# A Fourier transform along the tokens, followed by an expert layer: rows split by parity in place of halves

## The chip, the cores and the metric

The kernel runs on one core of one Trainium2 chip. The metric is the device time of one execution in microseconds, the median of several runs. Engines are named as in the profile: PE is TensorE (PEld its weight loads), DVE is VectorE, ACT is ScalarE, POOL is GpSimd, SP is SyncE, whose queue issues most DMA transfers.

## What is computed

The input x has 8 batches of 3072 tokens and 256 features, all in fp32; the weights come as float64.

```python
X = np.fft.fft(x, axis=1); X = np.fft.fft(X, axis=2)
x = X.real.astype(np.float32).reshape(8 * 3072, 256)
h = x @ w_in                                  # 256 x 2048
sp = np.where(h > 20.0, h, np.log1p(np.exp(np.minimum(h, 20.0))))
out = (h * np.tanh(sp)) @ w_out               # 2048 x 256
```

## The kernel before

**Tiling.** The 3072 tokens are taken as 3 x 1024. The transform of length 3 is made with additions, the one of length 1024 with matmuls against a table of cosines and sines (dft). The 1024 rows are folded to 256 with sums and differences (pair L332, sums L348 to L353, last_fold L362): tiles F0e, F1e, F0o, F1o, where "e" holds sums over features and "o" differences, and the digit c names one of two **halves** of the rows (0 to 127, and 256 down to 129). Row 128 has no partner. It is handled apart: make_mids (L627) computes its folds from a small tile ymid; put_mids (L374) places them by DMA in row 0 of fold tiles, nine transfers a batch; add_mid (L459) adds the rest.

**Even and odd frequencies.** For even frequencies the two halves are added before the matmul, for odd ones subtracted (over_c, L364, adds and subtracts the halves of the folds for one of the parities of each kind). A call of transform (L421) makes the cosine or sine sum of one parity into one PSUM tile: for even frequencies two matmuls of 128 and 130 columns (L429, L431), for odd ones two of 256 columns (L426), accumulated. The profile shows each of these fp32 matmuls as two passes.

**Chunks and steps.** The results of a batch are made as three chunks, each of 1024 tokens and 256 features, in the order first_chunk (L467), other_chunks (L491) and last_chunk (L521); each chunk is split into a high and a low part (split_to, L453: ScalarE copies the high part h, VectorE or GpSimd subtracts to get the low part l) for matmuls in reduced precision. The chunk is then multiplied with 16 blocks of the hidden layer, one block a step. A step (tau, L938 on) issues: six matmuls into pa and pb (mm1, L828 to L830); twelve matmuls of the output layer for the step six before (mm2, L869); make_h on VectorE (L837 to L839), which reads pa and pb; ScalarE's copy gh and GpSimd's difference gl of the step four before (L847, L848); ScalarE's Mish (L959). The first 12 steps use a plain fp32 path for mm2 (L860).

**What sets the order.** Every engine works its queue in the order in which the program issues. A batch has 48 steps. Steps 1, 2, 5 and 7 call other_chunks (steps 12 to 15 in batch 0), steps 17 and 18 last_chunk, steps 10 to 44 spread the folds of the next batch (fold_ops, L385, with a cost written by hand for each part), and steps 44 and 45 call first_chunk for the next batch, even and odd frequencies. pa and pb have two PSUM buffers each, and mm1 and the transforms take them in turn. So a transform's VectorE work has to be through before mm1 comes round to the same buffer.

**The start.** Batch 0's work before and among the first steps, and the conversion of the float64 weights (conv), stand in a list written by hand (EARLY, L153): entries with -1 come before step 0. chunk0 (L806) makes batch 0's first chunk, fold_z (L772) its folds, col_z (L672) and col_cs (L687) the same transforms for feature 0 of all batches, first_p0 (L705) that of batch 0 broadcast to all rows, and warm runs matmuls on zeros. The small arrays (ymid, ysel, eye, xcol in one tile, loaded) come on ACT's DMA queue (L724), the rest on SP's (L726 to L732).

Of the kernel before, what the change touches and what calls it, by code (L numbers as in the profile page):

```python
# [27 lines left out]
EVEN = list(range(2, 511, 4)) + list(range(0, 513, 4))  # L28
ODD = list(range(1, 512, 2))
NE = 258  # L30

DT = 2 * NE + 4 * 256
COLS0 = EVEN[:256] + ODD
COLS2 = EVEN[:128] + EVEN[129:] + ODD

# [30 lines left out]
def _layout(x, w_in, w_out):  # L66
# [6 lines left out]
    rows = np.array([[[_rows(n1, w, sg, 256 - m if c else m) for sg in range(2)] for n1 in range(3)]  # L73
# [3 lines left out]
    mids = np.array([_rows(n1, w, sg, 128) for w in range(2) for n1 in range(3) for sg in range(2)])  # L77
# [6 lines left out]
        "mid": np.ascontiguousarray(ym).reshape(12 * NB, D + 1),  # L84
# [5 lines left out]
def _tables():  # L90
# [10 lines left out]
    ev, od = np.array(EVEN), np.array(ODD)  # L101
    ae = 2 * np.pi * ((p[:, None] * ev[None, :]) % N2) / N2
    dft = np.zeros((128, DT))
    dft[:, :257] = np.cos(ae)
    dft[:, NE:NE + 257] = np.sin(ae)

    dft[0, :NE] *= 0.5
    dft[0, NE:2 * NE] = 0.0
    dft[0, NE:NE + 128] = np.sin(2 * np.pi * ((128 * ev[:128]) % N2) / N2)
    for c, m in enumerate((p, 256 - p)):  # L110
        ao = 2 * np.pi * ((m[:, None] * od[None, :]) % N2) / N2
        a8 = 2 * np.pi * ((128 * od) % N2) / N2
        o = 2 * NE + 512 * c
        dft[:, o:o + 256] = np.cos(ao)
        dft[:, o + 256:o + 512] = np.sin(ao)
        dft[0, o:o + 256] = np.cos(a8) if c else 0.5
        dft[0, o + 256:o + 512] = 0.5 * np.sin(ao[0]) if c else np.sin(a8)
# [6 lines left out]
    ysel = np.concatenate([np.kron(np.concatenate([f1, k * f1]), eye) for f1 in (fe, fo) for k in (1, -1)], 1)  # L124
# [9 lines left out]
SMALL = (D + 1, 12 * NB, 128, 24 * NB)  # L134
# [18 lines left out]
EARLY = [  # L153
    (-1, 'warm', (2,)),
# [24 lines left out]
    (-1, 'col_z', (0,)),  # L179
# [5 lines left out]
    (-1, 'chunk0', (1, 2)),  # L185
    (-1, 'pairs0', (0, 0, 'o')),
# [60 lines left out]
def fft_moe(ctx, tc, x, w_in, w_out, small_d, cs_d, dft_d, out, single_d):  # L247
# [28 lines left out]
    alt = cp.tile([128, NE], F32, name="alt")  # L276
# [19 lines left out]
    mid0 = small(1, 3 * 128, 2)  # L296
    loaded = small(128, sum(SMALL))
    ymid, ysel, eye, xcol = (loaded[:n, sum(SMALL[:i]):sum(SMALL[:i + 1])] for i, n in enumerate((12 * NB, 12 * NB, 128, 128)))
    xcol = xcol.rearrange("p (c w i b) -> p c w i b", c=2, w=2, i=6)
    xt = small(128, 12 * NB).rearrange("p (k c q b) -> p k c q b", k=2, c=2, q=3)  # L300
    xm = small(1, 6 * NB).rearrange("p (k q b) -> p k q b", k=2, q=3)
# [5 lines left out]
    mid_d = dp.tile([6 * NB, 2, 128], F32, name="mid_d")  # L307
# [13 lines left out]
    def fold_part(b, c, y, i, par):  # L321
        if par == 0 and c == 1:
            return folds[b][y, "-"] if (b, i) == (0, 0) else folds[b][1, y, 0][:, 0, 3 + i]
        return folds[b][c, y][:, par if COSINE[y][i] else 1 - par, i]
# [39 lines left out]
    def over_c(b, y, eng, lo=0):  # L364

        st, ops = folds[b], []
        ka = 0 if y == "e" else 1
        for k, i, j in ((ka, lo, 2), (1 - ka, 2, 3)):
            f0, f1, d = st[0, y][:, k, i:j], st[1, y][:, k, i:j], st[1, y, 0][:, 0, 3 + i:3 + j]
            ops.append(lambda f0=f0, f1=f1, d=d: eng.tensor_tensor(d, f0, f1, op=ALU.subtract))  # L370
            ops.append(lambda f0=f0, f1=f1: eng.tensor_tensor(f0, f0, f1, op=ALU.add))
        return ops

    def put_mids(b):  # L374


        for c, par, k, parts in ((0, 1, 0, (("o", 0), ("e", 2), ("o", 1))), (0, 0, 1, (("o", 0), ("e", 2), ("o", 1))),
                                 (1, 1, 1, (("e", 0), ("e", 1), ("o", 2)))):
            for y, i in parts:
                if b or i:  # L380
                    q, h = (i, 0) if y == "e" else ((i + 1) % 3, 1)
                    r = (3 * k + q) * NB + b
                    SP.dma_start(out=fold_part(b, c, y, i, par)[0:1], in_=mid_d[r:r + 1, h, :])

    def fold_ops(b):  # L385
# [20 lines left out]
        cross = []  # L406
        for i in range(4):
            def two(i=i):
                if i == 0:
                    cross.extend(zip(over_c(b, "e", V), over_c(b, "o", G)))  # L410
                for f in cross[i]:
                    f()
            steps.append((1.0, two))
# [3 lines left out]
    def const(c, par, sine):  # L417
        o = NE * sine if par == 0 else 2 * NE + 512 * c + 256 * sine
        return dft[:, o:o + (NE if par == 0 else 256)]

    def transform(dst, lhs, par, sine, mid_lhs=None, halves=(0, 1)):  # L421


        if par:
            for c in halves:
                T.matmul(dst, lhs(c), const(c, par, sine), start=c == 0, stop=c == 1)  # L426
        elif 1 in halves:
            t = const(0, 0, sine)
            T.matmul(dst[:, :128], lhs(1 - sine), t[:, :128], start=True, stop=True)  # L429
            d = dst[:, 128:NE]  # L430
            T.matmul(d, lhs(sine), t[:, 128:], start=True, stop=mid_lhs is None)  # L431
            if mid_lhs is not None:
                T.matmul(d, mid_lhs, alt[0:1, 128:], start=False, stop=True)
# [33 lines left out]
    def first_chunk(b, par, part=(0, 1, 2)):  # L467
# [10 lines left out]
        if 2 in part:  # L478
            if par == 0:
                new_chunk(ch)  # L480
# [542 lines left out]
```

## Time and profile before

| | |
|---|---|
| median of 3 runs | 1643.74 us (1643.66 to 1644.84) |
| profiled execution | 1645.03 us, span 1643.2 us |
| mean granted clock of TensorE | 0.995 of full |
| busy share PE, DVE, ACT, POOL | 99%, 66%, 52%, 70% |
| first step's first matmul | 35.02 us |

The span runs from the first to the last instruction. The timeline views give the start and the duration of instructions in us, and in brackets the idle time of the engine before one, with what ended it. Matmuls are pipelined: each shows some 0.17 us more than the time until the next may start, so the time a matmul costs is read from start to start.

### The profile page before, as it was taken

How to read it: one execution, taken by the hardware profiler on the slowest of the kernel's cores; microseconds unless marked ns; L12 is line 12 of the kernel's file. 1: busy time of each engine (PE TensorE's matmuls, PEld its weight loads, DVE VectorE, ACT ScalarE, POOL GpSimd, SP SyncE). 2: the span in 40 equal slices, each digit the busy share in tenths (PEclk: the TensorE clock that was granted, in tenths of full speed). 3: DMA queues.
4: the chain of work that ended last, by engine and by line, in shares of the span. 5: the costliest groups of instructions: out<-in, count | busy, mean ns of one | idle time of the engine just before them, and what ended most of it. 6: DMA issues, size and time to landing. Idle time of an engine off the chain costs nothing.

```text
span 1643.2 us, 20689 instructions
## 1 busy us (share of the span) xinstructions
PE 1629.2 (99%) x7484; PEld 1389.9 (85%) x7484; DVE 1085.3 (66%) x1612; ACT 849.9 (52%) x936; POOL 1148.4 (70%) x660
## 2 busy tenths in 40 slices
PE   8999999999999999999999999999999999999999
PEld 4557888888888888888888888888888888888887
DVE  6887776667666676676766767667766667664453
ACT  3445555555555555555554555555555555454454
POOL 2629876787658785687856886578865888565566
PEclk9999999999999999999999999999999999998999
DMA  5522002000030000300102000300002000000000
GB/s 240 206 77 90 1 33 93 17 32 27 7 110 0 33 26 7 109 33 1 33 24 86 33 3 31 109 1 33 26 7 109 23 11 27 7 33 26 7 27 26
DMA packets 24863, 74.96 MB, mean 46 GB/s; under 512 B 2981, under 2 KB 3106, under 8 KB 23738
## 3 DMA queue, kind: packets, MB, share of 16 engines
q1 hardware_dynamic: 24474, 73.03, 12.2%
q8 instruction: 60, 0.98, 0.3%
q10 hardware_dynamic: 288, 0.61, 0.1%
q14 instruction: 41, 0.34, 0.1%
HBM read 48.35 MB, written 25.27 MB: 45 GB/s over the span
## 4 chain that ended last, share of the span: by engine, by line
PE 94%; DVE 4%; DMA 1%; issue 0%; POOL 0%; ACT 0%; SPq 0%; DVEq 0%; POOLq 0%; ACTq 0%
PE acc L869 59%; PE pb L829 5%; PE pb L828 5%; PE pb L830 5%; PE pa L828 5%; PE pa L830 5%; PE pa L829 5%; PE pb L426 1%; PE pa L426 1%; PE acc L860 1%; DMA wring<-w_in_dram 0%; DMA swol<-w_in_dram 0%; DVE hring L838 0%; DMA hring<-small_dram 0%; DVE hring L837 0%
## 5 line engine op out<-in xcount | busy, mean ns | idle before, releaser
L848 POOL TENSOR_TENSOR gl<-hring,gh 128x1024 fp32r<-128x1024 f32 x372 | 887.2, 2385 | 409.1 <-ACT gh L847 404.1
L847 ACT CAST gh<-hring 128x1024 fp32r<-128x1024 f32 x372 | 389.7, 1048 | 659.1 <-PE acc L869 645.3
L869 PE MATMUL acc<-gh,woh 128*128 128x512 f32 x1488 | 564.9, 380 | 0.0
L869 PE MATMUL acc<-gh,wol 128*128 128x512 f32 x1488 | 564.8, 380 | 0.0
L837 DVE SCALAR_TENSOR_TENSOR hring<-p0b,wc,pa 128x512 f32<-128x512 f32 x384 | 286.4, 746 | 369.1 <-PE pa L830 359.6
L959 ACT ACTIVATE hring<-hring 128x1024 f32<-128x1024 f32 x384 | 404.2, 1053 | 41.6 <-DVE hring L839 41.6
L869 PE MATMUL acc<-gl,woh 128*128 128x512 f32 x1488 | 394.3, 379 | 0.0
L869 PEld LDWEIGHTS acc<-gl,woh 128*128 128x128 f32 x1488 | 281.6, 189 | 40.4 <-POOL gl L848 0.2
L869 PEld LDWEIGHTS acc<-gh,wol 128*128 128x128 f32 x1488 | 281.7, 189 | 40.4
L869 PEld LDWEIGHTS acc<-gh,woh 128*128 128x128 f32 x1488 | 281.7, 189 | 40.2
L838 DVE TENSOR_TENSOR hring<-hring,pb 128x512 f32<-128x512 f32 x384 | 264.0, 688 | 42.3 <-PE pb L830 1.4
L839 DVE TENSOR_TENSOR hring<-hring,pb 128x512 f32<-128x512 f32 x384 | 263.6, 686 | 13.3
L828 PE MATMUL pa<-h,wch 128*128 128x512 f32 x384 | 155.5, 405 | 0.0
L829 PE MATMUL pa<-l,wch 128*128 128x512 f32 x384 | 145.9, 380 | 1.2 <-DVE l L455 1.2
L828 PE MATMUL pb<-h,wsh 128*128 128x512 f32 x384 | 146.0, 380 | 0.8 <-ACT h L454 0.4
L829 PE MATMUL pb<-l,wsh 128*128 128x512 f32 x384 | 145.9, 380 | 0.3 <-POOL l L455 0.3
L830 PE MATMUL pa<-h,wcl 128*128 128x512 f32 x384 | 145.8, 380 | 0.0
L830 PE MATMUL pb<-h,wsl 128*128 128x512 f32 x384 | 145.8, 380 | 0.0
L829 PEld LDWEIGHTS pa<-l,wch 128*128 128x128 f32 x384 | 72.8, 190 | 12.5 <-issue 1.7
L828 PEld LDWEIGHTS pa<-h,wch 128*128 128x128 f32 x384 | 72.7, 189 | 12.2 <-issue 1.1
L828 PEld LDWEIGHTS pb<-h,wsh 128*128 128x128 f32 x384 | 72.7, 189 | 12.2 <-PE pa L830 1.2
L829 PEld LDWEIGHTS pb<-l,wsh 128*128 128x128 f32 x384 | 72.7, 189 | 10.9 <-POOL l L455 0.6
(275 smaller groups left out, 1163.5 us busy)
## 6 DMA issues: line engine op xcount, KB each, us to landing
xring<-x_dram SPq DMA_DIRECT2D x32, 768.0 KB
out_dram<-ot SPq DMA_DIRECT2D x96, 256.0 KB
p0b<-p_d SPq DMA_DIRECT2D x23, 256.0 KB
swoh<-w_in_dram SPq DMA_DIRECT2D x2, 1024.0 KB
swoh<-w_out_dram SPq DMA_DIRECT2D x2, 1024.0 KB
xring<-w_out_dram SPq DMA_DIRECT2D x2, 1024.0 KB
swol<-w_out_dram SPq DMA_DIRECT2D x2, 1023.5 KB
wring<-w_out_dram SPq DMA_DIRECT2D x2, 1023.5 KB
```

Of the source, the lines that this page charges most:

```text
L426: T.matmul(dst, lhs(c), const(c, par, sine), start=c == 0, stop=c == 1)
L828: T.matmul(dst, wh[:, fs], mixed(q[n + "h"]), start=True, stop=False)
L829: T.matmul(dst, wh[:, fs], mixed(q[n + "l"]), start=False, stop=False)
L830: T.matmul(dst, wl[:, fs], mixed(q[n + "h"]), start=False, stop=True)
L837: V.scalar_tensor_tensor(h[:, 0:512], p0b[ch], wc0[:, f:f + 1], pa, op0=ALU.mult, op1=ALU.add)
L838: V.tensor_tensor(h[:, 512:1024], h[:, 0:512], pb, op=ALU.add)
L839: V.tensor_tensor(h[:, 0:512], h[:, 0:512], pb, op=ALU.subtract)
L847: A.copy(gh, h)
L848: G.tensor_tensor(gl, h, gh, op=ALU.subtract)
L860: T.matmul(acc[i], w[:, o:o + 128], h[:, 512 * t:512 * t + 512], start=f == 0, stop=False)
L869: T.matmul(o, wout(w, f)[:, 128 * d:128 * d + 128], v, **kw)
L959: A.activation(hring[:, tau % RH], hring[:, tau % RH], AF.Mish)
```

## The change

Rows are split by **parity** (c = 0: rows 0, 2, 4, ...; c = 1: rows 1, 3, 5, ...) in place of halves. The transform of the even and of the odd rows is then made apart, each for half of the frequencies (130 columns for even frequencies, 128 for odd ones), side by side in one PSUM tile; the other half follows as sum and difference of the two (butterfly). over_c goes; put_mids has three transfers a batch. Batch 0's first chunk, col_z, col_cs and first_p0 use another routine (direct), which lets TensorE accumulate sums and differences, with negated folds (negs, xneg). In the start all loads become entries of EARLY, the small arrays first on SP's queue; col_z(0) moves behind chunk0. The diff, cut to its core:

```diff
+NQ = (130, 128)
+DT = 4 * sum(NQ)
...
-SMALL = (D + 1, 12 * NB, 128, 24 * NB)
+SMALL = (D + 1, 6 * NB, 128, 24 * NB)
...
 EARLY = [
+    (-1, 'load', ('small', 'S')),
+    (-1, 'load_w', ('in', 0)),
+    (-1, 'load', ('cs', 'A')),
+    (-1, 'load', (0, 'S')),
+    (-1, 'load', (1, 'S')),
+    (-1, 'load', ('dft', 'S')),
+    (-1, 'load', (2, 'S')),
+    (-1, 'load', (3, 'S')),
+    (-1, 'load_w', ('in', 1)),
     (-1, 'warm', (2,)),
...
-    (-1, 'col_z', (0,)),
     (-1, 'fold_z', (1,)),
     (-1, 'conv', ('out', 0, 0)),
     (-1, 'chunk0', (0, 1)),
     (-1, 'chunk0', (0, 2)),
     (-1, 'chunk0', (1, 1)),
     (-1, 'chunk0', (1, 2)),
+    (-1, 'col_z', (0,)),
...
     def put_mids(b):
-        for c, par, k, parts in ((0, 1, 0, (("o", 0), ("e", 2), ("o", 1))), (0, 0, 1, (("o", 0), ("e", 2), ("o", 1))),
-                                 (1, 1, 1, (("e", 0), ("e", 1), ("o", 2)))):
+        for y, i in (("o", 0), ("e", 2), ("o", 1)):
...
     def transform(dst, lhs, par, sine, mid_lhs=None, halves=(0, 1)):
+        n = NQ[par]
+        for c in halves:
+            mid = mid_lhs is not None and (par, sine, c) == (0, 0, 0)
+            T.matmul(dst[:, n * c:n * c + n], lhs(c), const(c, par, sine), start=True, stop=not mid)
...
+    def direct(dst, lhs, par, sine, mid_lhs=None, halves=(0, 1)):
+        n = NQ[par] - 1 + par
+        d = dst[:, :2 * n].rearrange("p (k s) -> p k s", k=2)
+        def twice(v):
+            return v[:, None, :].to_broadcast([v.shape[0], 2, n])
+        if 0 in halves:
+            T.matmul(d, lhs(0, False), twice(const(0, par, sine, 0, n)), start=True, stop=False)
+            if mid_lhs is not None and (par, sine) == (0, 0):
+                T.matmul(d, mid_lhs, twice(alt[0:1, :n]), start=False, stop=False)
+        if 1 in halves:
+            for k in (1, 0):
+                T.matmul(d[:, k], lhs(1, k == 0), const(1, par, sine, 0, n), start=False, stop=k == 0)
+
+    def butterfly(eng, dst, a, b, par, last=False):
+        lo, hi = (0, 128) if par else (0, 129) if last else (1, 129)
+        m = hi - lo
+        eng.tensor_tensor(dst[:, 0:m], a[:, lo:hi], b[:, lo:hi], op=ALU.subtract)
+        lo, hi = (1, 128) if last and not par else (0, 128)
+        eng.tensor_tensor(dst[:, m:256], a[:, lo:hi], b[:, lo:hi], op=ALU.add)
...
+    def first_chunk(b, par):
...
+        transform(pa, lambda c: fold_part(b, c, "e", 0, par), par, 0)
+        transform(pb, lambda c: fold_part(b, c, "o", 0, par), par, 1)
...
+        for k, p in enumerate((pa, pb)):
+            a = fp.tile([128, NQ[0]], F32, tag=f"base{k}", name="base")
+            both = fp.tile([128, 256], F32, tag=f"both{k}", name="both")
+            if k == par == 0:
+                add_mid(a[:, None, :n], p[:, None, :n], 0, b)
+                V.tensor_tensor(ends[:, b:b + 1], a[:, 0:1], p[:, n:n + 1], op=ALU.subtract)
+            else:
+                A.copy(a[:, :n], p[:, :n])
+            butterfly(V, both, a, p[:, n:2 * n], par)
+            split_to(q["pq"[k] + "h"][:, par], q["pq"[k] + "l"][:, par], both, V)
...
     def other_chunks(b, par, odd):
...
+        base = fp.tile([128, 2 * NQ[0]], F32, tag="base", name="base")
         if par == 0:
-            add_mid(base, pa, 1 + odd, b)
+            add_mid(base[:, None, :n], pa[:, None, :n], 1 + odd, b)
+            V.tensor_copy(base[:, n:2 * n], pa[:, n:2 * n])
         else:
-            V.tensor_copy(base[:, :n], pa[:, :n])
+            V.tensor_copy(base[:, :2 * n], pa[:, :2 * n])
         scaled, plain = (base, pb) if odd else (pb, base)
-        V.scalar_tensor_tensor(spare, scaled[:, :256], R3 if odd else -R3, plain[:, :256], op0=ALU.mult, op1=ALU.add)
...
-        split_to(q[h][:, par], q[l][:, par], spare, G)
-        V.scalar_tensor_tensor(full2[odd][:, sl].rearrange("p (a s) -> p a s", s=128), later(scaled, par),
-                               -R3 if odd else R3, later(plain, par), op0=ALU.mult, op1=ALU.add)
+        both = fp.tile([128, 256], F32, tag="both0", name="both")
+        for k, eng in ((0, V), (1, G)):
+            t = fp.tile([128, 2 * NQ[0]], F32, tag=f"turn{k}", name="turn")
+            V.scalar_tensor_tensor(t[:, :2 * n], scaled[:, :2 * n], R3 if odd != k else -R3, plain[:, :2 * n],
+                                   op0=ALU.mult, op1=ALU.add)
+            butterfly(eng, full2[odd][:, sl] if k else both, t, t[:, n:2 * n], par, k)
+        split_to(q[h][:, par], q[l][:, par], both, G)
...
     def make_mids():
...
-        for i, (o, v) in enumerate(((n + NB, od), (n + 4 * NB, od), (3 * NB, ev))):
-            T.matmul(pb[0:1, 128 * i + 128:128 * i + 256], ysel[:, o:o + 1], v, start=True, stop=True)
+        T.matmul(pb[0:1, 128:256], ysel[:, n + NB:n + NB + 1], od, start=True, stop=True)
...
-    G.memset(alt, 0.0)
...
-    A.dma_start(out=loaded, in_=small_d)
...
     def fold_z(c):
...
-            if c:
-                k = 0 if y == "e" else 1
-                f0, f1, d = folds[0][0, y][:, k, 0], folds[0][1, y][:, k, 0], eo[:, i, 0]
-                V.tensor_tensor(d, f0, f1, op=ALU.subtract)
-                V.tensor_tensor(f0, f0, f1, op=ALU.add)
...
+            for k, y in enumerate("eo"):
+                negs[y] = fp.tile([128, 2, 128], F32, tag=f"turn{k}", name="neg")
+                A.mul(negs[y], folds[0][1, y][:, :, 0], -1.0)
```

## Rows read from the trace of the kernel before

**Rows 1.** The page, part 1: engine, busy us (share), instructions.

```profile
PE 1629.2 (99%) x7484; PEld 1389.9 (85%) x7484; DVE 1085.3 (66%) x1612; ACT 849.9 (52%) x936; POOL 1148.4 (70%) x660
```

**Rows 2.** Chain in order of time, 400 to 425 us: start, us, what.

```profile
403.13 0.22 PE pa L828
...
407.01 0.22 PE pa L828
```

**Rows 3.** The same chain, 0 to 110 us.

```profile
0.73 6.17 DMA hring<-small_dram
```

**Rows 4.** Line L459: count, min/median/max ns, first and last start us, form.

```profile
L459 DVE SCALAR_TENSOR_TENSOR base<-alt,midc,pa x24: 472/483/486, 33.2 to 1442.9; 128x258 f32<-128x258 f32 x24
```

**Rows 5.** TensorE's timeline, even transform: start, us, line, op, out<-in, count.

```profile
1401.88 0.38 PE L429 MATMUL pa<-dft,e 128*128 128x128 f32 x2
...
1402.98 0.38 PE L829 MATMUL pa<-l,wch 128*128 128x512 f32 x1
```

**Rows 6.** TensorE's timeline, odd transform of the same chunk.

```profile
1406.65 0.59 PE L426 MATMUL pa<-dft,F0e 128*128 128x256 f32 x2
...
1408.60 0.38 PE L829 MATMUL pa<-l,wch 128*128 128x512 f32 x1
```

**Rows 7.** VectorE's timeline behind the even transform; idle before in brackets.

```profile
1402.52 0.48 DVE L459 SCALAR_TENSOR_TENSOR base<-alt,midc,pa 128x258 f32<-128x258 f32 x1 [1.35 <-PE pa L431]
1403.60 1.46 DVE L455 TENSOR_TENSOR l<-base,h 128x256 fp32r<-128x256 f32 x1 [0.59 <-ACT h L454]
1404.98 0.41 DVE L455 TENSOR_TENSOR l<-pb,h 128x256 fp32r<-128x256 f32 x1
1405.31 0.14 DVE L489 COPY ends<-base 128x1 f32<-128x1 f32 x1
...
1406.93 0.69 DVE L839 TENSOR_TENSOR hring<-hring,pb 128x512 f32<-128x512 f32 x1
```

**Rows 8.** GpSimd's timeline there, and behind the next even transform.

```profile
1400.86 0.45 POOL L371 TENSOR_TENSOR F0o<-F0o,F1o 128x128 f32<-128x128 f32 x1
1402.39 2.38 POOL L848 TENSOR_TENSOR gl<-hring,gh 128x1024 fp32r<-128x1024 f32 x1 [1.09 <-ACT gh L847]
1407.17 2.37 POOL L848 TENSOR_TENSOR gl<-hring,gh 128x1024 fp32r<-128x1024 f32 x1 [2.40 <-ACT gh L847]
...
1424.43 2.39 POOL L848 TENSOR_TENSOR gl<-hring,gh 128x1024 fp32r<-128x1024 f32 x1 [1.51 <-ACT gh L847]
```

**Rows 9.** ScalarE's timeline at the first of them.

```profile
1403.18 0.39 ACT L454 CAST h<-base 128x256 fp32r<-128x256 f32 x1
```

**Rows 10.** VectorE's timeline behind the even transform of another chunk.

```profile
1424.57 0.48 DVE L459 SCALAR_TENSOR_TENSOR base<-alt,midc,pa 128x258 f32<-128x258 f32 x1 [1.35 <-PE pa L431]
...
1425.84 0.74 DVE L837 SCALAR_TENSOR_TENSOR hring<-p0b,wc,pa 128x512 f32<-128x512 f32 x1
```

**Rows 11.** TensorE's timeline, 0 to 36 us.

```profile
1.85 3.78 PE L770 MATMUL warm<-zero 128*128 128x512 f32 x4 [1.85 <-POOL zero L764]
7.27 0.66 PE L635 MATMUL pa<-early,hring 96*48 96x128 f32 x2 [1.64 <-DVE early L630]
...
8.71 1.44 PE L640 MATMUL pb<-early,hring 96*1 96x128 f32 x6
...
15.64 2.74 PE L746 MATMUL pa<-xring,hring 128*128 128x512 f32 x6
...
35.02 0.48 PE L828 MATMUL pa<-h,wch 128*128 128x512 f32 x1
```

**Rows 12.** VectorE's timeline, 0 to 38 us.

```profile
7.34 0.68 DVE L569 TENSOR_SCALAR wgl<-swoh 128x1024 int32<-128x1024 int32 x1
...
31.81 0.29 DVE L782 TENSOR_TENSOR F0o<-F0o,F1o 128x128 f32<-128x128 f32 x1
```

**Rows 13.** TensorE's waits from 36 us on: total, times, longest.

```profile
PE pa L829 <- DVE l L455: 1.2, 1, 1.2
```

**Rows 14.** VectorE's timeline, 100 to 106 us.

```profile
100.52 0.28 DVE L370 TENSOR_TENSOR e<-F0e,F1e 128x128 f32<-128x128 f32 x1
```

More of the change, by code (lines that the diff above doesn't have):

```diff
@@ L72, in _layout @@
     m = np.arange(128)
-    rows = np.array([[[_rows(n1, w, sg, 256 - m if c else m) for sg in range(2)] for n1 in range(3)]
+    rows = np.array([[[_rows(n1, w, sg, 2 * m + c) for sg in range(2)] for n1 in range(3)]
                      for c in range(2) for w in range(2)]).transpose(0, 3, 1, 2)
@@ L100, in _tables @@
     p = np.arange(128)
[L101 to L117, printed above, removed]
+    parts = []
+    for par in range(2):
+        i = np.arange(NQ[par])
+        freq = 2 * i + par
+        for g in (np.cos, np.sin):
+            for c in range(2):
+                t = g(2 * np.pi * ((2 * p[:, None] + c) * freq[None, :] % N2) / N2)
+                if c == 0:
+                    t[0] *= 0.5
+                    if par and g is np.sin:
+                        t[0] = 1.0 - 2.0 * (i % 2)
+                t[:, 129:] = 0.0
+                parts.append(t)
+    dft = np.concatenate(parts, 1)
     eye = np.eye(NB, dtype=f)
@@ L405, in fold_ops, with const @@
                 steps.append((1.5, lambda c=c, k=k: [last_fold(b, c, y, eng, k) for y, eng in (("e", V), ("o", G))]))
[L406 to L413, printed above, removed]
         steps.append((0.0, lambda: put_mids(b)))
         return steps
-    def const(c, par, sine):
-        o = NE * sine if par == 0 else 2 * NE + 512 * c + 256 * sine
-        return dft[:, o:o + (NE if par == 0 else 256)]
+    def const(c, par, sine, lo=0, hi=None):
+        o = 4 * NQ[0] * par + NQ[par] * (2 * sine + c)
+        return dft[:, o + lo:o + (NQ[par] if hi is None else hi)]
@@ L677, in col_z @@
         pa = ps("pa")
-        transform(pa[:NB, :n], lambda c: xt[:, par, c, 0], par, 0, xm[:, 0, 0] if par == 0 else None)
-        A.copy(placed(r)[:, par], pa[:NB, :256])
+        direct(pa[:NB], lambda c, neg: (xneg if neg else xt)[:, par, c, 0], par, 0, xm[:, 0])
+        A.copy(placed(r)[:, par], span(pa[:NB], par))
         if par == 0:
-            A.copy(pe, pa[:NB, 256:257])
+            A.copy(pe, pa[:NB, 0:1])
             SP.dma_start(out=pe_d, in_=pe)
@@ L801, in sums0, with load @@
             f()
-        if c == 1 and hi == 7:
-            for f in over_c(0, y, eng, 1):
-                f()
+    def load(name, queue):
+        eng = SP if queue == "S" else A
+        dst, src = {"small": (loaded, small_d), "cs": (cs, cs_d), "dft": (dft, dft_d)}.get(name) or (xring[:, name], x[0, name])
+        eng.dma_start(out=dst, in_=src)
     def chunk0(par, part):
-        first_chunk(0, par, (part,))
+        st = folds[0]
+        if part == 0:
+            st["ps", par] = ps("pa"), ps("pb")
+        for k, (p, y) in enumerate(zip(st["ps", par], "eo")):
+            if part < 2:
+                direct(p, lambda c, neg: negs[y][:, 1 - par if k else par] if neg else fold_part(0, c, y, 0, par), par, k, None, (part,))
+                continue
+            if par == k == 0:
+                new_chunk(0)
+                base = fp.tile([128, 2 * NQ[0]], F32, tag="base", name="base")
+                v = [t[:, 0:258].rearrange("p (k s) -> p k s", k=2) for t in (base, p)]
+                add_mid(*v, 0, 0)
+                V.tensor_copy(ends[:, 0:1], base[:, 0:1])
+                p = base
+            split_to(*(chunks[0]["pq"[k] + e][:, par] for e in "hl"), span(p, par), V)
     parts = dict(chunk0=chunk0, put_mids=lambda: put_mids(0))
     parts.update({g.__name__: g for g in (
-        make_mids, warm, first_p0, sum_n1, add_n1, fold_z, pairs0, sums0, load_w, conv, make_wc, make_w0, make_wl, split_out, col_fold, col_z, col_cs)})
+        make_mids, warm, first_p0, sum_n1, add_n1, fold_z, pairs0, sums0, load, load_w, conv, make_wc, make_w0, make_wl, split_out, col_fold, col_z, col_cs)})
     early = {}
```

174 lines of the change are left out of this document (60 added, 114 removed).

## The prediction

> **What bounds the kernel now.** The page's first part has TensorE busy for 99% of the span [rows 1]. In the chain in order of time, one step's first matmul starts at 403.13 and the next step's at 407.01 [rows 2]: a step of 18 matmuls takes 3.88 us, and the chain there lies on TensorE alone, so whatever TensorE is spared in such a stretch is gained. The other stretch is the start. There the chain begins with the load of the small arrays, from 0.73 for 6.17 us to 6.90 [rows 3], goes on over TensorE, and after that lies mostly on VectorE until the first dozen steps are through. The two stretches are priced apart.
>
> **Transforms on TensorE.** A pair of transforms, even then odd, stands three times in a batch; L459, once for each even one, runs 24 times [rows 4]. An even one is now 4 matmuls of 128 or 130 columns, each in two passes. It begins at 1401.88; the second matmul of the step behind it starts at 1402.98 [rows 5]; less the 0.22 of that step's first matmul, the transform takes 0.88 us, 0.11 a pass. An odd one is 4 matmuls of 256 columns: 1406.65 to 1408.60, less 0.22, is 1.73 us [rows 6]. After the change an even one is 4 matmuls of 130 columns (0.88, as now) and an odd one 4 of 128 (0.88 too: the same count and shape as the even one's). A pair falls by 1.73 - 0.88 = 0.85 us. Batch 0's first pair is made by other code in the start, so 23 pairs: **-19.5 us**.
>
> Bounds of that price: a pass of half the columns can't take less than half an odd pass of now (0.22 / 2 = 0.11), so no more is to be had; if the weight load stopped hiding behind so short a pass, a pass could take 0.22, the odd transform would stay at 1.73 and nothing would be saved. I take 0.88, since the even rows have that shape.
>
> The Trainium skill, "TensorE: Matmul & The Clock Gate", section "The mechanism" of Part 3, says that a weight load overlaps a running matmul only where the two use different rows of the array. Here every matmul uses all 128 rows, so by that rule the saving would be nothing. The trace speaks against it: 0.11 a pass leaves no room for a load of its own.
>
> **Work behind the transforms.** What TensorE no longer combines, VectorE does, and it must empty the PSUM buffers pa and pb (two of each) before TensorE comes round to them. I walk the first chunk of the next batch (steps 44 and 45 of a batch), where most is added, with today's durations.
>
> Today, even part: base from 1402.52 for 0.48, l from base and h from 1403.60 for 1.46, l from pb from 1404.98 for 0.41, ends for 0.14, and right behind it make_h, whose last operation starts at 1406.93 and takes 0.69 [rows 7]. The 1.46 is a wait: GpSimd's gl runs from 1402.39 for 2.38, to 1404.77 [rows 8], and l, with both inputs in SBUF, ends 0.28 after it. l from pb, with one input in PSUM, takes its plain 0.41.
>
> After: an operation of 128 columns with an input in PSUM has no row; it lies between 0.14 (one column) and 0.41 (256) [rows 7], and I take the middle, 0.28. Base with 130 columns is then 0.35 (0.48 less 0.13), ends 0.14, difference and sum 0.28 each with an overlap of 0.08 as between today's rows: done at 1403.55. h takes ScalarE 0.39 [rows 9]. l waits for gl and ends at 1405.05. Then come the second half's difference and sum, to 1405.46, its h, to 1405.88, and its l, now with both inputs in SBUF, 1405.91 to 1406.33 if GpSimd is idle then; its next gl starts at 1407.17 [rows 8]. make_h (2.25) follows to 1408.50. The shorter odd transform begins at 1406.65 and ends at 1407.53, and the step after it wants the pb that make_h reads three matmuls of 0.22 later, at 1408.18: TensorE waits **0.3 us**. In the odd part ScalarE's activation stands ahead of the new copy out of PSUM, so the sums come at 1409.8 to 1411.6; pb is free then, and the step that takes it starts at about 1411.8: no wait. 7 batches: **+2.1 us**. Bounds: nothing, if an operation costs 0.14; 1.5 us a batch (+10.5) if each costs 0.41 and the overlap is lost (four operations by 0.13 and four overlaps of 0.08, some 0.9 more, and as much again for odd).
>
> In the other chunks VectorE starts at 1424.57 and reaches make_h at 1425.84 [rows 10]. After: base 0.35, a copy of 0.28, 0.41 for the multiply-add, then difference and sum of SBUF data, held until gl ends (1424.43 + 2.39 = 1426.82 [rows 8]) and done at 1427.17, then 0.41 for the second multiply-add: make_h starts at 1427.43, 1.6 late, and ends at 1429.7. TensorE wants that pb at about 1430.2 (3.88 after the even transform's end, then 0.88 and 0.65). The cover is 0.5 us, so I take nothing; were it gone, each of 16 pairs would pay its lateness. GpSimd gets two operations of 128 columns there (0.45 today at 1400.86 [rows 8]) and waits for VectorE before them, but it has two steps until gl is read. The over_c operations and the six of nine put_mids transfers that go lie beside TensorE's work: nothing gained. The last fold moves to step 43, to where GpSimd's 1400.86 row stands; with three times the columns it ends by 1402.2, and the pb matmuls that read it start half a transform after 1401.88, at 1402.3: nothing again, with 0.1 of cover.
>
> **The start.** The small arrays move ahead of all on SP's queue. Today they land at 6.90 and make_mids' matmuls begin at 7.27, though the warm-up matmuls were through at 1.85 + 3.78 = 5.63 [rows 3, 11]. After, TensorE's own order binds; the warm-up starts some 0.3 earlier (one memset less): make_mids at about 5.3, -2.0. What they are moved past: w_in 0 lies behind 320 KB, but conv starts at 7.34 today, behind make_mids on VectorE [rows 12]; x and dft are read from 15.64 on [rows 11], and dft is a third smaller. make_mids loses 4 of 16 passes (six take 1.44 [rows 11], some 0.2 each): -0.8. fold_z loses four VectorE operations of 0.29 [rows 12]: -1.2. Sum **-4.0 us**, between 0 (another wait takes over) and -6.1: a warm-up pass takes some 0.9 today, a pass of the x sums 0.43 [rows 11], the two clock levels (1.2 and 2.4 GHz); should the higher be granted earlier, up to 2.1 come on top. col_z, moved behind chunk0, now stands right before the first step: 4 passes of 258 columns and 4 of 129, at the low level at most 4 x 0.43 + 4 x 0.22 = 2.6. TensorE waits 1.2 for l there today [rows 13], which covers half; the other 1.4 is set against the clock. Later on VectorE's chain over_c's four operations of 0.28 go [rows 14]: **-1.0**. col_cs gets one operation more: **+0.3**. ScalarE's two negations (0.39 each by rows 9) run beside VectorE.
>
> **Sum.** -19.5 + 2.1 - 4.0 - 1.0 + 0.3 = -22.1. The profiled execution took 1645.03, so 1622.9; it lies 1.3 above the median of the three runs, 1643.74, for which the sum gives 1621.6. About 0.2% (3.3 us) is what a measurement of this kernel can tell from no change.
>
> **Rivals.**
> 1. The start gains nothing and the first chunk costs 1.5 a batch: -19.5 + 10.5 - 1.0 + 0.3 = -9.7, 1634. For it: the start passes through many hands, any of which may take the place of the wait removed, and two prices have no row. Against: the 1.2 us during which GpSimd is idle. All between this and the forecast is counted here: 0.20.
> 2. Slower: the second l of the first chunk's even part misses GpSimd's idle stretch. It has 1.2 us (1405.91 against 1407.17); from there on gl holds it to 1407.17 + 2.37 + 0.28 = 1409.82, make_h ends at 1412.0, and TensorE, wanting pb at 1408.2, waits 3.8: 7 x 3.8 = 26.6 in place of 2.1, 1646. For it: today's rows show such a hold each batch. Against: the operations ahead of it would have to be twice as long as walked: 0.05.
> 3. The change does not do what it says: passes don't shrink, since the load shows. 1643.7 - 4.0 - 1.0 + 0.3 = 1639, or no change if the start gives nothing either. Against: the even passes of 0.11 [rows 5]: 0.05.
> 4. No wait in the first chunk and the higher clock early: -19.5 - 6.1 - 1.0 + 0.3 = -26.3, 1617.4: 0.12.
> The forecast: 0.58. Range: from 1616, just below rival 4, to 1634, rival 1. Slower is rival 2, 0.05; within 0.2% the worse part of rival 3, 0.03; faster the rest, 0.92.
>
> **What would show it.** Right: odd transforms of about 0.9 us; TensorE waiting some 0.3 for make_h after step 45's transform; make_mids' first matmul near 5.3; the first step near 31 (today 35.02 [rows 11]). Wrong: passes of 0.2 us; an l of the first chunk of over 2 us; waits of TensorE on VectorE of over 1 us in every batch; a first step as late as now.

## The result, and the profile after

The changed kernel takes **1625.12 us** (median of 4 runs, 1624.29 to 1630.86) against 1644.29 for the kernel before beside it: ratio **0.9886**, 95% interval 0.9866 to 0.9906. The forecast was 1621.6, range 1616 to 1634. Run twice more later, it took 1631.05 and 1625.24; the median of all twelve executions is 1625.97. They do not spread evenly: 8 lie between 1624.29 and 1628.55, 4 between 1630.86 and 1631.25. That spread turned out to be half of the lesson, so three traces of the same program are read below.

From the trace, the first matmul of every step's mm1 gives the time by stretches (spans 1643.2 and 1622.6):

| stretch, us | before | after | difference | foretold |
|---|---|---|---|---|
| start of the first step | 35.02 | 30.08 | -4.9 | -4.0 |
| batch 0 | 215.07 | 214.20 | -0.9 | -2.95 |
| batches 1 to 6, each | 194.34 | 192.38 | -1.96 | -2.25 |
| batch 7 to the end | 227.10 | 224.05 | -3.05 | -1.7 |

The page's first part, as in [rows 1]; VectorE gained 101 instructions and 34 us, TensorE lost 22 us:

```profile
PE 1607.2 (99%) x7510; PEld 1374.2 (85%) x7510; DVE 1118.9 (69%) x1713; ACT 861.2 (53%) x956; POOL 1155.0 (71%) x684
```

TensorE's timeline at the first chunk of a next batch, which answers to [rows 5, 6]: the start of the even transform, that of the odd one, and the step behind it.

```profile
1384.60 0.39 PE L409 MATMUL pa<-dft,F0e 128*128 128x130 f32 x2
...
1389.38 0.38 PE L409 MATMUL pa<-dft,F0e 128*128 128x128 f32 x2
...
1390.19 0.46 PE L825 MATMUL pa<-h,wch 128*128 128x512 f32 x1
1390.49 0.38 PE L826 MATMUL pa<-l,wch 128*128 128x512 f32 x1
1390.71 0.38 PE L827 MATMUL pa<-h,wcl 128*128 128x512 f32 x1
1391.39 0.45 PE L825 MATMUL pb<-h,wsh 128*128 128x512 f32 x1 [0.30 <-DVE hring L836]
1391.68 0.38 PE L826 MATMUL pb<-l,wsh 128*128 128x512 f32 x1
```

Read from start to start as in the prediction, the odd transform takes 1390.49 - 1389.38 - 0.22 = 0.89 us; it took 1.73. Behind it there is a new wait: the matmul into pb starts 0.68 after the one before it, where 0.22 is usual, and the next follows after 0.29. That is 0.53 us lost. VectorE and GpSimd show why, as in [rows 7, 8]:

```profile
1385.25 0.35 DVE L466 SCALAR_TENSOR_TENSOR base<-alt,midc,pa 128x130 f32<-128x130 f32 x1 [1.35 <-PE pa L409]
...
1386.66 1.12 DVE L462 TENSOR_TENSOR l<-both,h 128x256 fp32r<-128x256 f32 x1 [0.47 <-ACT h L461]
1387.71 0.27 DVE L435 TENSOR_TENSOR both<-base,pb 128x128 f32<-128x128 f32 x1
...
1388.65 0.42 DVE L462 TENSOR_TENSOR l<-both,h 128x256 fp32r<-128x256 f32 x1 [0.47 <-ACT h L461]
...
1390.56 0.69 DVE L836 TENSOR_TENSOR hring<-hring,pb 128x512 f32<-128x512 f32 x1
```
```profile
1385.12 2.38 POOL L845 TENSOR_TENSOR gl<-hring,gh 128x1024 fp32r<-128x1024 f32 x1 [0.54 <-ACT gh L844]
1389.90 2.37 POOL L845 TENSOR_TENSOR gl<-hring,gh 128x1024 fp32r<-128x1024 f32 x1 [2.40 <-ACT gh L844]
```

The first l is held until gl ends (1385.12 + 2.38 = 1387.50, then 0.28), the second pair waits behind it, and the second l falls into GpSimd's idle 2.40 us and takes its plain 0.42. make_h ends at 1391.25 and TensorE goes on at 1391.39. TensorE's waits from 28 us on, in place of [rows 13] (total, times, longest); the last two are of step 16 of batch 0, read in experiment 4:

```profile
PE pb L825 <- DVE hring L836: 2.8, 8, 0.7
...
PE pb L826 <- POOL l L462: 1.0, 1, 1.0
PE pb L825 <- ACT h L461: 1.0, 1, 1.0
```

The start of TensorE, answering to [rows 11], first in this profiled execution (1624.44 us), then in another execution of the same program (1631.00 us):

```profile
1.46 3.78 PE L756 MATMUL warm<-zero 128*128 128x512 f32 x4 [1.46 <-POOL zero L750]
5.33 0.62 PE L637 MATMUL pa<-early,hring 48*24 48x128 f32 x2
...
7.05 3.17 PE L756 MATMUL warm<-zero 128*128 128x512 f32 x6
10.06 2.74 PE L732 MATMUL pa<-xring,hring 128*128 128x512 f32 x6
...
30.08 0.48 PE L825 MATMUL pa<-h,wch 128*128 128x512 f32 x1
```
```profile
5.18 0.62 PE L637 MATMUL pa<-early,hring 48*24 48x128 f32 x2
...
7.61 5.91 PE L756 MATMUL warm<-zero 128*128 128x512 f32 x6
13.31 1.98 PE L732 MATMUL pa<-xring,hring 128*128 128x512 f32 x4
...
34.79 0.48 PE L825 MATMUL pa<-h,wch 128*128 128x512 f32 x1
```

make_mids starts at 5.3 or 5.2 (before: 7.27), TensorE does the same work without a gap, and yet the six warm-up passes take 3.17 us in one and 5.91 in the other: the higher clock level was granted from 6.13 us on in one and from 13.49 on in the other. The windows view over 28 to 34 us (PE busy and granted clock) has the other half; the first row is of the 1624.44 us execution, the second of the 1631.00 us one, and the kernel before shows 0.50 there too:

```profile
28.00:34.00 6.00, 5.51 (x26) 1.00 0.01 0
```
```profile
28.00:34.00 6.00, 5.42 (x22) 0.50 0.01 3
```

So of the 4.9 us by which the first step came earlier in the first profile, 4.7 are absent in the second.

### The profile page after: what moved, and what is told of

Same layout as the page of the kernel before. It is cut to its first block, busy times and chain, and to the rows that moved or that the text cites. A ratio compares the mean times of both kernels' runs of the same rounds, so it can differ in the third digit from the quotient of the medians.

```text
span 1622.6 us, 20886 instructions
## 1 busy us (share of the span) xinstructions
PE 1607.2 (99%) x7510; PEld 1374.2 (85%) x7510; DVE 1118.9 (69%) x1713; ACT 861.2 (53%) x956; POOL 1155.0 (71%) x684
## 4 chain that ended last, share of the span: by engine, by line
PE 91%; DVE 5%; DMA 2%; ACT 1%; issue 1%; POOL 0%; SPq 0%; DVEq 0%; POOLq 0%
PE acc L866 58%; PE pb L825 5%; PE pb L826 5%; PE pb L827 5%; PE pa L825 5%; PE pa L827 5%; PE pa L826 5%; PE pa L409 1%; PE acc L857 1%; DMA swol<-w_out_dram 1%; PE pb L409 1%; DVE hring L834 1%; DVE hring L835 1%; DVE hring L836 1%; DVE l L462 0%
```

## The experiments

Each comparison is with the kernel before on the same chip, as a ratio with its 95% interval.

**1. Is it TensorE's columns?** The kernel before, with the odd matmuls cut to 128 columns. It leaves half of the odd transforms' work out; nothing else of the change is in it.

```diff
-                T.matmul(dst, lhs(c), const(c, par, sine), start=c == 0, stop=c == 1)
+                d = dst[:, 128 * c:128 * c + 128]
+                T.matmul(d, lhs(c), const(c, par, sine)[:, :128], start=True, stop=True)
```

> The kernel before, with each odd transform's matmuls of 256 columns cut to 128: each half of the rows makes one half of the columns, so half of the odd transform's work is left out, and VectorE's work stays as before. Theory A, TensorE's columns are the price: an odd transform takes 0.89 in place of 1.73, a batch falls from 194.34 to 191.8, the execution by 24 x 0.84 = 20 us to about 1623.5. Rival, weight loads show behind short passes: passes of 0.2 us, the batch stays at 194. Rival, the steps are held by VectorE anyway: the batch falls by less than 2.

Measured: 1623.07, ratio 0.9872 (0.9857 to 0.9887), or -21.9 us. Batches 1 to 6 take 191.84 each, 2.5 less than before, or 0.83 a pair, and the first step stands at 34.80, as before. TensorE's timeline of a step behind a short odd transform: no wait ahead of pb, since VectorE has its old work.

```profile
1389.64 0.39 PE L427 MATMUL pa<-dft,F0e 128*128 128x128 f32 x2
...
1390.97 0.38 PE L831 MATMUL pa<-h,wcl 128*128 128x512 f32 x1
1391.18 0.38 PE L829 MATMUL pb<-h,wsh 128*128 128x512 f32 x1
```

Of the 21.9, batches 1 to 6 give 15.0. Batch 7 of this trace (222.24, before 227.10) holds more than its two pairs, 1.7: the lower clock lasted 3.4 us there in place of 10.2, so some 3 us of the gain in this trace are the clock. Fewer columns alone are worth more than what the whole change gains in batches 1 to 6 (2.50 each against 1.96); what VectorE now does for it costs the difference.

**2. The new wait.** The changed kernel, with both pairs of difference and sum ahead of both splits in first_chunk: while l would wait for gl, VectorE makes the second pair out of PSUM. ScalarE's copy of the second half moves ahead of its h with it.

```diff
         q = chunks[ch]
+        sums_of = []
         for k, p in enumerate((pa, pb)):
...
+            sums_of.append((a, both, p))
+        for k, (a, both, p) in enumerate(sums_of):
             butterfly(V, both, a, p[:, n:2 * n], par)
+        for k, (a, both, p) in enumerate(sums_of):
             split_to(q["pq"[k] + "h"][:, par], q["pq"[k] + "l"][:, par], both, V)
```

> The changed kernel; in first_chunk both sums and differences are made before either split, so they fill the time in which VectorE waits for GpSimd's gl. Theory A, TensorE's wait behind step 45 comes from make_h being late behind the second l: make_h starts about 1 us earlier, the step after the odd transform takes 3.97 in place of 4.50, a batch 191.9 in place of 192.4, the execution 7 x 0.5 = 3.5 us less, about 1621. Rival, the wait comes from ScalarE's order (activation ahead of the copies out of PSUM) or from the buffers: the step stays at 4.5 and the time at 1624.4.

Measured: 1622.8, ratio 0.9876 (0.9856 to 0.9897); batches 1 to 6 take 191.85, 0.53 less than the changed kernel's. VectorE's timeline: the two l follow on each other at gl's end (1381.63 + 2.39 = 1384.02 in this trace), and make_h ends (1386.12 + 0.69 = 1386.81) before TensorE wants pb at 1387.43.

```profile
1382.90 0.28 DVE L437 TENSOR_TENSOR both<-base,pb 128x128 f32<-128x128 f32 x1
1383.17 1.47 DVE L462 TENSOR_TENSOR l<-both,h 128x256 fp32r<-128x256 f32 x2
...
1386.12 0.69 DVE L840 TENSOR_TENSOR hring<-hring,pb 128x512 f32<-128x512 f32 x1
```
```profile
1387.43 0.38 PE L829 MATMUL pb<-h,wsh 128*128 128x512 f32 x1
```

The wait was the order of VectorE's own operations around gl, 7 x 0.53 = 3.7 us in the trace. The timed difference to the changed kernel's 1625.97 is 3.2, but that is between chips, and the four executions here lie between 1620.38 and 1627.58; what shows the cause is the same step of each batch in the trace.

**3. The order of the loads, from both sides.** The kernel before with the small arrays first on SP's queue, and the changed kernel with them on ScalarE's queue as before.

```diff
-    A.dma_start(out=loaded, in_=small_d)
+    SP.dma_start(out=loaded, in_=small_d)
+    load_w("in", 0)
     A.dma_start(out=cs, in_=cs_d)
-    load_w("in", 0)
```
```diff
-    (-1, 'load', ('small', 'S')),
-    (-1, 'load_w', ('in', 0)),
+    (-1, 'load', ('small', 'A')),
     (-1, 'load', ('cs', 'A')),
+    (-1, 'load_w', ('in', 0)),
```

> The kernel before, with only the small arrays moved first on SP's queue (w_in 0 behind them, cs still on ACT's queue). Theory A: make_mids starts near 5.4 in place of 7.27, the first step near 31.5 to 32.5 in place of 35.02, the execution 2.5 to 3.5 us shorter, about 1640.5. Theory B: under 1 us.

> The changed kernel, with the small arrays and cs back on ACT's DMA queue as before (they land late, sharing the DMA engines with w_in). Theory A, the start was won by the small arrays' place: make_mids' first matmul goes from 5.33 back to about 7, TensorE's higher clock level is granted some microseconds later than 6.13, the first step starts at 33 or later (30.08 in the changed kernel) and the execution takes some 3 us more, 1627 to 1628. Theory B, the start was won by the shorter make_mids and fold_z alone: the first step stays before 31 and the time within 1 us of the changed kernel's 1624.4.

The first: 1640.76 (10 runs), ratio 0.9976 (0.9967 to 0.9985), 4.2 us less than the median before on that chip (1644.92); make_mids at 5.56, the first step at 30.28. The second: 1629.2, ratio 0.9905 (0.989 to 0.992); make_mids at 7.11, the first step at 34.47. Four executions of the second, 1627.64 to 1630.37, lie inside the changed kernel's spread. Taken together the two seemed to give the loads the whole start, until the control of experiment 4 showed the changed kernel itself with a first step at 34.79.

**4. Batch 0, the output weights, and a control**, on one chip.

> The changed kernel itself, run again beside the three below, so that they are compared on one chip. Expected: a median near 1625 us, batches 1 to 6 of 192.4 us each from first step to first step, the first step's first matmul near 30.1. If the ratio to the kernel before is off 0.9886 by more than 0.001, small differences between kernels of one chip and another are not to be read.

Measured: 1631.05, ratio 0.9901 (0.9869 to 0.9933). The ratio is off 0.9886 by 0.0015, more than the 0.001 set for it, so small differences between kernels on different chips are not to be read. Steps and batches 1 to 6 agree (192.38 to 192.40); the start does not, as shown above. The kernel before has the same low stretch (28.05 to 34.88 there, 27.15 to 33.97 here), so these two traces compare the start at like clock. The first step's start is moved by only 0.2, but before, its second matmul waited 1.2 us for l [rows 13], and that is gone: the second step starts at 38.90 before and 37.25 here, 1.65 earlier. The x sums start 2.33 earlier (15.64, 13.31), so 0.7 was lost between them and the second step: the way to the first step grew by 2.1 (19.38 to 21.48), and the wait that is gone gives back 1.4. In this run what grew lies on TensorE: first_p0 takes 3.50 us (24.53 to 28.03) where it took 2.79 (26.73 to 29.52), TensorE waits for the negated folds, and col_z's 2.24 us of matmuls stand whole between 32.55 and the first step. VectorE's base, which also has to come ahead of col_z, is through at 31.78, while the matmuls of chunk0 still run. TensorE's timeline and base:

```profile
29.25 0.80 PE L428 MATMUL pa<-dft,neg 128*128 128x129 f32 x2 [0.58 <-ACT neg L771]
...
31.99 0.63 PE L428 MATMUL pb<-dft,neg 128*128 128x128 f32 x2
32.55 1.03 PE L423 MATMUL pa<-dft,hring 128*8 128x258 f32 x2
```
```profile
29.08 2.31 DVE L572 TENSOR_SCALAR swol<-swol 128x1024 int32<-128x1024 int32 x1
31.31 0.47 DVE L466 SCALAR_TENSOR_TENSOR base<-alt,midc,pa 128x258 f32<-128x258 f32 x1
```

In the first profile (1624.44 us), at the higher level, TensorE is through with chunk0 sooner and VectorE sets the first step. The conversion of the output weights (L572, 0.69 usually) waits 0.43 for their landing and is then held by GpSimd's first fold of batch 1, base comes after it, and TensorE waits 1.22 for base; the timelines of GpSimd, VectorE and TensorE, in this order:

```profile
25.30 2.19 POOL L335 TENSOR_TENSOR o<-xring 128x768 f32<-128x768 f32 x1 [16.07 <-DVE F1o L765]
```
```profile
26.25 1.79 DVE L572 TENSOR_SCALAR swol<-swol 128x1024 int32<-128x1024 int32 x1 [0.43 <-DMA swol<-w_out_dram]
27.96 0.47 DVE L466 SCALAR_TENSOR_TENSOR base<-alt,midc,pa 128x258 f32<-128x258 f32 x1
```
```profile
28.48 0.60 PE L423 MATMUL pa<-dft,hring 128*8 128x258 f32 x2 [1.22 <-DVE base L466]
```

Two edits follow. The conversion goes behind col_z:

```diff
-    (-1, 'conv', ('out', 0, 0)),
     (-1, 'chunk0', (0, 1)),
...
     (-1, 'col_z', (0,)),
+    (-1, 'conv', ('out', 0, 0)),
```

> The changed kernel, with the first part of the conversion of the first output weights moved from ahead of the last pieces of batch 0's first chunk to behind col_z(0). In the trace of the changed kernel VectorE waits there for the landing of those weights (26.22 us), then needs 1.8 us for one operation, and base, which releases col_z's matmuls, starts at 27.96 only. Theory A (this load is the new bound of the start): base starts at about 26.9, right behind TensorE's transform, and the first step's first matmul comes 1.0 to 1.7 us earlier, at 28.4 to 29.1; VectorE pays the two operations later (1.4 us ahead of the first make_h), so the time falls by 0 to 1.5 us. Rival B (it only moves the wait): the first step is earlier but the second and third steps are later by as much, batch 0 grows by what the first step gained, and the time is unchanged at about 1625.

Measured: 1623.33, ratio 0.9869 (0.9843 to 0.9896). base starts at 27.12, but in the traced execution TensorE was at the lower level from 23.25 to 30.07, and its own matmuls set the first step, 31.40: undecided there. In the traced execution of the three edits together (below) there was no low stretch, and from the x sums to the first step it took 18.74 us (11.99, 30.73) against 20.02 in the changed kernel (10.06, 30.08): 1.3 earlier, as theory A had it; TensorE no longer waits for base there. The second step keeps 1.1 of it (21.36 after the x sums against 22.48), against rival B. That compares one trace of each.

The other edit gives batch 0's sums and differences to GpSimd, because VectorE's timeline of the changed kernel shows two of them held, by GpSimd's conversion and by its split:

```profile
103.51 2.41 POOL L580 TENSOR_TENSOR xring<-xring 128x1024 f32<-128x1024 f32 x1 [1.77 <-DVE xring L577]
105.88 2.40 POOL L624 TENSOR_TENSOR wol<-swoh,woh 128x1024 fp32r<-128x1024 f32 x1
```
```profile
104.53 1.53 DVE L435 TENSOR_TENSOR both<-turn 128x128 f32<-128x128 f32 x1
105.99 2.43 DVE L437 TENSOR_TENSOR both<-turn 128x128 f32<-128x128 f32 x1
```
```diff
-            butterfly(eng, full2[odd][:, sl] if k else both, t, t[:, n:2 * n], par, k)
+            butterfly(eng if b else G, full2[odd][:, sl] if k else both, t, t[:, n:2 * n], par, k)
```

The Trainium skill, "SBUF — State Buffer", section "Who interferes with whom", says that a VectorE operation with two SBUF inputs contends with a GpSimd operation that reads SBUF, and that the one that comes later stands still until the other is through. The rows agree: 0.29 us of work takes 1.53 and 2.43, each until GpSimd's operation has ended.

> The changed kernel, with the sum and difference of batch 0's other chunks (four of them: two parities, two chunks) made by GpSimd alone; in the trace of the changed kernel VectorE made half of them in step 13 of batch 0, and was held for 1.5 and 2.4 us by GpSimd's conversion and split of the output weights. Theory A (VectorE's operations with two SBUF inputs are what GpSimd holds, and batch 0 lost its advantage there): VectorE's two long operations are gone, steps 14 to 16 of batch 0 fall from 5.8, 6.6 and 7.0 us to about 5.7 each, batch 0 shrinks from 214.2 to about 212.2, the time by about 2 us, to near 1623. Rival B (GpSimd's own queue is what is late: its four extra operations wait behind the conversion, and the chunk's low part comes no earlier): batch 0 stays at 214 or grows to 215 to 217, since the low part is needed by the same step; the time is unchanged or 1 to 3 us longer.

Measured: 1623.43, ratio 0.9866 (0.9842 to 0.9891). Steps 14 and 15 fall from 5.82 and 6.57 to 5.62 each and batch 0 from 214.20 to 212.79, 1.4 of the 2 expected. Step 16 stays at 6.95: there TensorE waits 1.42 for h and 0.59 for l of the chunk made one step earlier, which the new sum and difference deliver later than before (5.74 then).

> The changed kernel with three edits at once: in the first chunk both pairs of sum and difference come ahead of both splits (as tried before by itself), batch 0's other sums and differences go to GpSimd, and the first output weights' conversion is moved behind col_z(0). If the gains add (theory A of each): batches 1 to 6 of 191.85 us, first step at 28.4 to 29.1, batch 0 near 212, and a time of 1625 - 3.7 - 2 - 1 = 1618 us. If batch 0 is set by VectorE's and GpSimd's whole work there rather than by these waits (rivals B): only the first edit counts, 1621 to 1622.

Measured: 1621.87, ratio 0.9859 (0.983 to 0.9888). Batches 1 to 6 take 191.85. The time is that of rivals B, and theory A's 1618 did not come. Batch 0 took 214.46, not 212: in the traced execution the lower clock was granted from 119.65 to 123.06, within step 16, which took 8.66.

**5. Chance or cause in the start**, and the best version, on one chip.

> The changed kernel once more, with more runs, beside two kernels that differ from it in the first 10 us alone. Its eight times so far fall into two groups, 1624.3 to 1626.1 (four) and 1630.9 to 1631.3 (four), and the two traces taken differ in the start: with the higher clock granted from 6.13 on the first step's first matmul came at 30.08 (1624.44 us), with 13.49 at 34.79 (1631.00 us), though make_mids started at 5.33 and 5.18. Theory A (the early start of make_mids lets the higher clock come early, in most executions): a median of 1624 to 1627, most times in the lower group. Rival B (the clock comes early or late by chance, whatever the loads): times spread over both groups, and the kernel with the loads as before, beside it, has the same mix.

> The changed kernel with the loads in the order of before (small arrays, then cosines, on ScalarE's queue), again, with more runs. The first time its median of 1629.2 lay between the two groups of the changed kernel, so it could not be told from it. Theory A: TensorE's idle 1.9 us ahead of make_mids (7.11 in place of 5.2) keeps or takes back the lower clock, and its median lies 2 to 4.5 us above that of the changed kernel beside it. Rival B (chance alone): the medians lie within 1.5 us of each other.

> The same kernel with late small arrays, but one of the second group's two warm-up matmuls moved ahead of make_mids, so that TensorE has no idle time while it waits for the small arrays; the number of warm-up matmuls is unchanged. Theory A (the idle gap costs, not the lateness): make_mids starts at about 7.1 as in the kernel beside it, TensorE's idle time ahead of it is below 0.3 us, the higher clock is not taken back around 9 us, and the median comes to within 1.5 us of the changed kernel's. Rival B (the small arrays are what the start waits for): the median stays with the loads as before, 2 to 4.5 us above the changed kernel's.

The last is the kernel with late small arrays and

```diff
-    (-1, 'warm', (2,)),
+    (-1, 'warm', (3,)),
     (-1, 'make_mids', ()),
-    (-1, 'warm', (2,)),
+    (-1, 'warm', (1,)),
```

Measured: 1625.24, ratio 0.9886 (0.9869 to 0.9902), for the changed kernel; 1628.22, 0.9911 (0.9896 to 0.9926), with the loads as before; 1628.25, 0.9907 (0.9892 to 0.9922), without the gap. The traces of the second and third:

```profile
7.44 0.40 PE L637 MATMUL pa<-early,hring 48*24 48x128 f32 x2 [2.19 <-DVE early L632]
...
8.79 4.75 PE L756 MATMUL warm<-zero 128*128 128x512 f32 x6
13.38 1.88 PE L732 MATMUL pa<-xring,hring 128*128 128x512 f32 x4
```
```profile
7.10 0.40 PE L637 MATMUL pa<-early,hring 48*24 48x128 f32 x2 [0.51 <-DVE early L632]
...
8.45 2.31 PE L756 MATMUL warm<-zero 128*128 128x512 f32 x4
10.60 2.74 PE L732 MATMUL pa<-xring,hring 128*128 128x512 f32 x6
```

With the gap, make_mids' passes run at the higher level, then the level is taken back (lower from 9.27 to 12.69; in experiment 3 from 9.22 to 12.64) and the x sums start at 13.38. Without the gap there is no such fall, and the first step stands at 30.63. That is as the idle-gap theory said, but the median did not follow: 1628.25 is 3 us above the changed kernel's, as rival B had it. One trace a kernel cannot say what its other executions did. All executions of the changed kernel with the loads as before, eight, have a median of 1628.8 and a mean of 1629.1, against 1625.97 and 1627.4 for its twelve; they overlap widely and come from several chips. So the place of the small arrays is shown to count in the kernel before (experiment 3); in the changed kernel some 3 us are likely, but not shown, and the path stays open. The third trace of the changed kernel is between the other two (x sums at 12.31, first step at 32.34, 1628.55 us). The edits of experiments 2 and 4 and the two versions with several edits leave the first 10 us as they are, so there are eight traces of one and the same start: the higher level came from 5.14, 6.13, 6.18, 6.37, 10.42, 11.07, 13.49 and 13.64 us on. With the gap, in two traces, it was granted near 5.8 us, taken back, and granted again from 12.64 and 12.69 on. An early start of make_mids goes with an early clock in half of these traces; what decides it is open.

> The changed kernel with the two edits that shortened a stretch in their own traces: sums and differences ahead of the splits in the first chunk (TensorE's wait of 0.53 us in each of 7 batches went), and batch 0's on GpSimd (batch 0 went from 214.2 to 212.8). If they add: batches 1 to 6 of 191.85 us, batch 0 of about 212.8, and a median 5 us below that of the changed kernel beside it, 1620 to 1622, whatever the start does in either. If the first step's time varies by 5 us as in the control, a difference of the medians between 2 and 8 us.

Measured: **1621.18**, ratio 0.9864 (0.9848 to 0.9881), 4.1 us below the changed kernel beside it. Batches 1 to 6 take 191.85, steps 14 and 15 of batch 0 5.62, batch 0 214.31 where 212.8 was expected. By their medians this and the version with three edits are the fastest of the whole computation, 1.4% below the kernel before; they can't be told apart from each other, nor by their intervals from each edit alone. Step 16 met the lower clock here too (122.87 to 126.28, 8.66 us); why it did in both of these and not where batch 0's edit stood alone is open.

## Why the prediction came out as it did

- **Transforms on TensorE, -19.5: right.** A pair of steps with its transforms fell by 0.83 us where 0.85 was foretold, so -19.1 for 23 pairs; experiment 1 has the same 0.83 without the rest of the change. Rival 3 fell: the odd transform's eight passes take 0.11 each. The Trainium skill, "TensorE: Matmul & The Clock Gate", section "The mechanism" of Part 3, says that a weight load overlaps a running matmul only where the two use different rows of the array. The trace does not agree at these shapes: 0.11 a pass. Nor did a saving of nothing follow from that rule: a load added to every pass, long or short, would have left the saving by columns.
- **The wait in the first chunk, +2.1: right in place and cause, too small.** The walk foretold the end of make_h 1.85 after the start of the odd transform; it is 1.87 (1391.25 - 1389.38). But TensorE restarted only 0.14 after that end, and its first pass then took 0.29 in place of 0.22. So 0.53 a batch, +3.7. The wait up to the end of make_h was foretold rightly (0.3); the mistake was to let a waiting matmul start at the instant its release comes, and at full speed. Rival 2's hold of the second l did not come: GpSimd was idle for it.
- **The other chunks, nothing: right.** VectorE's timeline behind an even transform, answering to [rows 10]:

```profile
1407.01 0.35 DVE L466 SCALAR_TENSOR_TENSOR base<-alt,midc,pa 128x130 f32<-128x130 f32 x1 [1.36 <-PE pa L409]
...
1408.14 1.25 DVE L435 TENSOR_TENSOR both<-turn 128x128 f32<-128x128 f32 x1
...
1409.86 0.73 DVE L834 SCALAR_TENSOR_TENSOR hring<-p0b,wc,pa 128x512 f32<-128x512 f32 x1
```

  One operation is held by gl, and make_h starts 2.85 after base (foretold 2.86). It lasts 2.25, to 1412.1; TensorE's next matmul into pb starts at 1412.68, a cover of 0.6 (foretold 0.5).
- **The start, -4.0: the sum was near, the working was not.** make_mids came 1.94 earlier (7.27 to 5.33; -2.0 foretold), and its passes gave 0.6 of 0.8: from make_mids to the x sums it takes 5.34 in the kernel before with the small arrays first (5.56, 10.90) and 4.73 in the changed one (5.33, 10.06). But from the x sums to the first step it takes 19.38 before and 20.02 or 21.48 in the two traces of the changed kernel. fold_z's 1.2 came on VectorE (its conversion starts 16.38 after the x sums before, 15.17 in the 1631.00 us execution) and not on TensorE. Three terms stood in its way. The larger first_p0, +0.7, was not in the sum. The negated folds, which were to run beside VectorE, kept TensorE waiting 0.58 or 0.75. Of col_z's matmuls half was to be covered, and they stand whole before the first step. In the first profile the conversion behind GpSimd's fold came on top.

  Two traces price this at like clock: the kernel before with the small arrays first (higher level from 6.23, lower from 23.30 to 30.13) and experiment 4's edit for batch 0, whose start is the changed kernel's (6.37, 23.43 to 30.26). Their first steps start at 30.28 and 31.50, their second at 34.15 and 33.96. So by the second step all of the change but the loads gained 0.2 where 2.0 was foretold (-0.8 and -1.2), and the loads alone gained 4.75 in the kernel before (38.90 to 34.15) where 2.0 was foretold. That the two errors nearly cancel is luck. The higher clock early stood in rival 4 as an extra 2.1: between the two traces of the changed kernel it made 4.7. In the trace without it the first step gained 0.2 and the second 1.65, between the forecast and rival 1's "the start gains nothing".
- **over_c in batch 0, -1.0: wrong.** From the second step's start on, batch 0 grew by 0.55 (211.19 to 211.74), though its three pairs saved 1.96 (with the first chunk's wait). The prediction took away VectorE's old operations there and put the new ones at nothing by the walk of a later batch, where no conversion stands: their two SBUF inputs meet GpSimd's conversion and split, and the chunk made in step 15 is wanted in step 16. col_cs's +0.3 was about right: the second step, which holds it, grew by 0.37.
- **Batch 7**: two pairs, -1.7 foretold; -1.3 and -1.4 in the later two traces. The -3.05 of the first has a low clock stretch of 6.8 us there in place of 10.2.

At like clock (the kernel before against the 1631.00 us execution) the change is worth 14.0 us of span: 11.75 in batches 1 to 6, 1.65 at the second step, 1.3 in batch 7, less 0.7 in the rest of batch 0. The other 6.6 between that execution and the first profile comes with the clock, 4.7 of it in the start and 1.7 in batch 7. So of the 22.1 foretold 14.0 came without an early clock, and the median, 19.2 below the one before, owes the rest to executions with a better clock, which the sum had not counted on.

## What to carry to other kernels

Halving the columns of these matmuls paid in full in the stretches that TensorE bounds (0.83 us a pair at 128 columns); the bill came on the engine that now combines the halves. Walk that engine's order around its long neighbour: here operations that read PSUM ran beside GpSimd's long ones (0.28 us), those with two SBUF inputs were held (1.12 and 1.25), so put the former first (0.53 us a batch). And trace a changed kernel more than once before a gain in the start is believed: one trace gave the first step 4.9 us, a second one of the same program 0.2.

## What was not expected of the hardware

- The same program, with TensorE's work without a gap from 1.5 to 13 us, got the higher clock from 6.13, 11.07 or 13.49 us on, and its first step started at 30.08, 32.34 or 34.79; in the last of these the lower clock was granted again from 27.15 to 33.97.
- A VectorE operation with a single SBUF input (L572, 128x1024 int32) took 1.79 and 2.31 us while GpSimd's L335 ran, and 0.69 or 0.75 elsewhere. The same section of the Trainium skill says that such a one-input operation can take both ports and then contends too; the rows agree.
